# Later bits for the second head, zero products in the head, and output tiles in the activation buffers: a bucketed attention with two feed-forward layers

## The chip, the cores and the metric

The kernel runs on one core of a Trainium2 chip. The metric is the device time of one execution in microseconds. Three runs of the kernel before took 791.81, 792.76 and 794.22 us; the median, 792.76, stands for it.

## The reference

Three stages follow each other. The attention has 2 batches of 8 heads, 768 tokens and 64 features a head. A query attends only to the keys in its own bucket; a bucket is the pattern of the signs of six projections. Two feed-forward layers of 1536 tokens x 512 features x 2048 hidden units come behind it, with different activations.

```python
q_bits = (einsum('bhsd,dk->bhsk', q, proj) > 0)         # the same for k
mask = q_bucket[..., :, None] == k_bucket[..., None, :]  # bucket = sum(bits * 2**i)
scores = where(mask, q @ k.T / sqrt(64), -1e9)
attn = exp(scores - max); attn = attn / (sum(attn) + 1e-9)
x = (attn @ v)                                  # heads side by side: 1536 x 512
h = x @ moe_w_in;  x = (h * tanh(softplus(h))) @ moe_w_out
h = x @ moe2_w_in; out = (h - tanh(h)) @ moe2_w_out
```

## The kernel before, in words

All products are split: every operand is kept as a high part in TensorE's rounded float format and a low part that holds the rest, and high x high, low x high and high x low are summed.

*Attention.* Heads are taken in eight pairs. For a pair, `load` brings k, q and v, `halves_split` makes the high and low parts (ql, kl and so on), and `piece` multiplies them by the projection planes (L412 to L414, three matmuls into a PSUM tile y). `bits` then turns y into signs: on VectorE for k, on ScalarE for q (L397, L395). The signs of both heads go into a tile z. For the first pair alone, the first head's signs are also written directly into its operand tiles (c and d, by a second `bits` on the same y), and `first_stack` copies the rest of that head's operands on the engines. All other heads get their operands a, b, c, d by DMAs from these tiles (`stack`), issued from SyncE; d<-z and c<-z are the two that need z.

A head is worked off in two halves of the queries, a half in three tiles of 128 queries. `scores` multiplies (L507, L508) into the PSUM tile s, of which there is one; VectorE clamps it and takes its minimum (L511), and ScalarE takes the exponential and its sum (L533). Scores 1, 3 and 5 of the whole program (`SPLIT_S`) use two single-bank PSUM tiles instead. `chunk` is called for six chunks of 128 keys a half: three transposes (L554) put the chunk into a PSUM tile pt, ScalarE casts it to the high part ph (L567), VectorE forms the low part pl (L570), or GpSimd does both for a few chunks (L559, L563), and two matmuls multiply ph and pl by the values (L578, L579). There are three tiles each for ph and pl, two for GpSimd's chunks, and six PSUM tiles with the tag pt, which y, the transposes, the products' sum and later the hidden layer share. `gather` adds the two halves of a product's rows (L586, L589), and `finish` divides by the sums (rden, L602 and L607) and splits the result into xh and xl.

*Feed-forward.* `feed_forward` goes over three blocks of 512 tokens for each layer; a block takes 16 hidden tiles: `hidden` (12 matmuls, L756 to L758), the activation (`mish`, or `shrink` with tanh into an f buffer, L791), the split into ph and pl, and `outer` (12 matmuls, L815) into four sums; two of these are the halves of s. In the second layer the sums are copied to osb buffers, of which there are two (L865, the last tile in two halves, L862), and stored. `convert` turns the double-precision weights into high and low float parts on VectorE, ScalarE and GpSimd.

*The order.* Each piece of work is an `op` with an engine, a booked cost, a key and the tiles it reads and writes. `Plan.order` lays all ops out by these costs: on each engine the one that can start first, and among equals the one with the lowest key. A result is taken to reach another engine after a booked latency (`LATE`, 0.25 us, for ScalarE, VectorE and GpSimd); `release` holds an op back to a time of this plan. The instructions are then written in that order, and each engine works its own list strictly in it. Keys are times too: chunk c of item n has `at(6n + c)`, a tick being 1.16 us, and a product had the key of its chunk plus `PV_LAG` = 4.0.

Ahead of the plan, VectorE clears a tile and casts it into `hot`, and seven matmuls of zeros (L900, `WARM`) run on TensorE.

Of the kernel before, what the change touches and what calls it, by code (L numbers as in the profile page):

```python
# [27 lines left out]
F32 = mybir.dt.float32  # L28
# [15 lines left out]
POOL_LAST = ((4,), (4,))  # L44
SPLIT_S = (1, 3, 5)
TAIL = 3
WARM = 7


G_BUFS, E_BUFS, GX_BUFS, F_BUFS = 3, 3, 2, 4  # L50
T_BUFS, O_BUFS, P_BUFS, U_BUFS = 3, 2, 6, 3

EPS = 0.005
SPARE = 1
LATE = 0.25
LATS = 0.15
LATC = 1.0
LATG = 0.6  # L60
# [5 lines left out]
T_ATT = 6.0  # L66
M0 = 6.0
AHEAD = 8
PV_LAG = 4.0
PIECE = 2.5  # L70
STACK = 11
VALUES = 11
# [1 line left out]
FIRST = (0.0, 1.0, 2.0, 6.0)  # L74
V_REL = 14.0
Q_REL = 8.0
OUT_LAG = 13.0
RAW = 12.0
C0 = 6.0
# [28 lines left out]
class Plan:  # L108
# [11 lines left out]
    def buf(self, pool, tag, shape, dtype=F32):  # L120
        return Buf(self, pool, tag, shape, dtype)
# [107 lines left out]
def tile_lsh_attention_moe(  # L229
# [63 lines left out]
    )  # L293
    ctx.enter_context(
        memory("left", (
            ("const", "", 1), ("xy", "", 1), ("wa", slots(0, N_A), 1), ("osb", "osb", O_BUFS), ("t", "t", T_BUFS),
            ("g", "ph", G_BUFS), ("e", "pl", E_BUFS), ("f", "f", F_BUFS),
        ))
    )
# [9 lines left out]
    xh = [xy_p.tile([P, B * S], F32R, name=f"xh{kk}") for kk in range(KD)]  # L309
    xl = [xy_p.tile([P, B * S], F32R, name=f"xl{kk}") for kk in range(KD)]  # L310

    zero = plan.pools["osb"].tile([P, XB], F32, tag="osb", name="zero")
    hot = plan.pools["osb"].tile([P, XB], F32R, tag="osb", name="hot")

    def x_tok(which, kk, t0, n):
        return [(which, kk, t) for t in range(t0, t0 + n)]
# [16 lines left out]
    def at(tick):  # L333
        return T_ATT + tick * TICK
# [57 lines left out]
    def bits(nm, out, y, r):  # L392

        if nm == "q":
            nc.scalar.activation(out=out, in_=y[r, :HB], func=AF.Sign, bias=zb[r], scale=-1.0)  # L395
        else:
            nc.vector.tensor_scalar(  # L397
                out=out, in0=y[r, :HB], scalar1=zb[r], scalar2=zs[r], op0=ALU.is_gt, op1=ALU.mult
            )

    def piece(g, nm, half, key):

        if (g, "z") not in stacks:
            stacks[g, "z"] = buf("z", "z", [64, S], F32R)
        z, (th, tl) = stacks[g, "z"], stacks[g, nm]
        c = slice(half * HB, (half + 1) * HB)
        y = buf("ps_t", "pt", [P, 512])
        r0 = 0 if nm == "k" else 32

        def planes():  # L410
            o = y()[:64, :HB]
            nc.tensor.matmul(o, pjh, th()[:, c], start=True, stop=False)  # L412
            nc.tensor.matmul(o, pjl, th()[:, c], start=False, stop=False)
            nc.tensor.matmul(o, pjh, tl()[:, c], start=False, stop=True)  # L414

        op("PE", 0.53, key + 0.3, planes, [(th, half), (tl, half)], [y])
        eng, cost = ("ACT", 0.55) if nm == "q" else ("DVE", 0.59)
        if g == 0:
            dst = stacks[0, 0][3 if nm == "k" else 2]
            rb = slice(r0, r0 + NR)  # L420
            op(eng, cost, key + 0.4, lambda: bits(nm, dst()[0:NR, c], y(), rb), [y], [(dst, "bits", half)])
        r = slice(r0, r0 + 2 * NR)
        op(eng, cost, key + 0.4, lambda: bits(nm, z()[r, c], y(), r), [y], [(z, nm, half)])

    def stack(g, h, key):

# [47 lines left out]

    def values_in(g, h, key):
        vt = buf("vt", "vt", [P, NT, 2 * D], F32R)
        hi, lo = (slice(0, D), slice(D, 2 * D))[::1 if h == 0 else -1]
        raw = raws[g, "v"]
        op(
            "POOL", 0.5, key, lambda: pool_copy(vt()[:, :, hi], raw()[:, h]), [raw], [(vt, 0)],  # L480
            release=0.0 if g else V_REL,
        )
        op(
            "POOL", 0.97, key + 0.1,
            lambda: nc.gpsimd.tensor_tensor(
                out=vt()[:, :, lo], in0=raw()[:, h], in1=vt()[:, :, hi], op=ALU.subtract
            ),
            [raw, (vt, 0)], [(vt, 1)],
        )
        vts[g, h] = vt  # L490
# [47 lines left out]
        )  # L538
        return p

    def chunk(g, h, half, c, ps, o, key):
# [9 lines left out]
        def transpose():  # L551
            for t in range(TB):
                pc = ps[t]().rearrange("p a b -> p (a b)")
                nc.tensor.transpose(pt()[:, t * P:(t + 1) * P], pc[:, c * P:(c + 1) * P], ident)  # L554

        op("PE", 0.41, key, transpose, ps, [pt])
        if pooled:
            pf = buf("f", "f", [P, XB])
            op("ACT", 0.38, key + 0.1, lambda: nc.scalar.copy(pf()[:, w], pt()[:, :HB]), [pt], [pf])  # L559
            op("POOL", 0.5, key + 0.2, lambda: pool_copy(ph()[:, w], pf()[:, w]), [pf], [ph], lat=LATG)  # L560
            op(
                "POOL", 0.97, key + 0.3,
                lambda: nc.gpsimd.tensor_tensor(out=pl()[:, w], in0=pf()[:, w], in1=ph()[:, w], op=ALU.subtract),  # L563
                [pf, ph], [pl], lat=LATG,
            )
        else:
            op("ACT", 0.38, key + 0.1, lambda: nc.scalar.copy(ph()[:, w], pt()[:, :HB]), [pt], [ph])  # L567
            op(
                "DVE", 0.47, key + 0.2,
                lambda: nc.vector.tensor_tensor(  # L570
                    out=pl()[:, w], in0=pt()[:, :HB], in1=ph()[:, w], op=ALU.subtract
                ),
                [pt, ph], [pl],
            )

        def product():
            vc = vt()[:, c, :]
            nc.tensor.matmul(o()[:, :HB], vc, ph()[:, w], start=(c == 0), stop=False)  # L578
            nc.tensor.matmul(o()[:, :HB], vc, pl()[:, w], start=False, stop=(c == NT - 1))  # L579

        op("PE", 0.35, key + PV_LAG, product, [(vt, 0), (vt, 1), ph, pl], [o])

    def gather(h, o, u, key):
        main, rest = slice(h * D, (h + 1) * D), slice((1 - h) * D, (2 - h) * D)
# [55 lines left out]
    for g in range(len(pairs)):  # L640
        load(g)
        k0 = at(TICKS * (g - 1)) if g else 0.0
        if g == 0:
            clear_stack()
        else:
            for n, nm in enumerate("kq"):
                halves_split(g, nm, (0, 1), k0 + PIECE * n * TICK)
        for n, (nm, half) in enumerate((("k", 0), ("q", 0), ("k", 1), ("q", 1))):
            key = k0 + PIECE * n * TICK if g else FIRST[n]
            if g == 0:  # L650
                halves_split(0, nm, (half,), key)
            piece(g, nm, half, key)
            if g == 0:
                first_stack(half, nm, key + 0.35)
        for h in range(2):
            if g or h:
                stack(g, h, k0 + STACK * TICK if g else 5.0)
            values_in(g, h, k0 + (VALUES + 2 * h) * TICK)
        us = []
        for half in range(2):  # L660
            sums[g, half] = buf("small", "sums", [P, 2, TB])
            us.append(buf("u", "u", [P, HB]))
        for h in range(2):
            for half in range(2):
                n = (2 * g + h) * 2 + half
                ps = [
                    scores(g, h, half, t, at(NT * n + 2 * t - AHEAD) + 0.3) for t in range(TB)
                ]
                o = buf("ps_t", "pt", [P, 512])
                for c in range(NT):  # L670
                    chunk(g, h, half, c, ps, o, at(NT * n + c))
                gather(h, o, us[half], at(NT * (n + 1)) + PV_LAG)
                if h == 1:
                    finish(g, half, us[half], at(NT * (n + 1)) + PV_LAG + 0.3)


    wb_es = ExitStack()
# [144 lines left out]
    def feed_forward(which, j, first):  # L822
# [17 lines left out]
        for d, (a, n) in enumerate(acc):  # L840
# [13 lines left out]
            else:  # L854
                b, t = divmod(j * TX + d, NT)
                rows = out[b * S:(b + 1) * S, :].rearrange("(t p) d -> t p d", p=P)[t]
                osb = buf("osb", "osb", [P, DM])
                eng, cost, e = (("ACT", 0.48, nc.scalar.copy), ("DVE", 0.6, nc.vector.tensor_copy))[d % 2]
                if tail and d == KD - 1:
                    for i in range(2):  # L860
                        c = slice(i * hm, (i + 1) * hm)
                        op("ACT", 0.26, key, lambda osb=osb, a=a, n=n, c=c: nc.scalar.copy(osb()[:, c], a()[:, n, c]), [(a, n)], [(osb, i)])  # L862
                        dma(P * hm * 4, key, lambda rows=rows, c=c: rows[:, c], lambda osb=osb, c=c: osb()[:, c], [(osb, i)], [("out", j, d, i)])
                    continue
                op(eng, cost, key, lambda osb=osb, a=a, n=n, e=e: e(osb(), a()[:, n, :]), [(a, n)], [osb])  # L865
                dma(P * DM * 4, key, lambda rows=rows: rows, osb, [osb], [("out", j, d)])
# [26 lines left out]

    nc.scalar.dma_start(out=cst, in_=cst_d)
    nc.scalar.preload_act_table_set("natural_log_exp_and_others")
    nc.vector.memset(zero, 0.0)
    nc.vector.tensor_copy(hot, zero)
    for _ in range(WARM):
        o = plan.pools["ps_t"].tile([P, XB], F32, tag="pt", name="hot_ps")
        nc.tensor.matmul(o, hot[:, 0:P], hot, start=True, stop=True)  # L900
# [61 lines left out]
```

## Time and profile before

| | us |
|---|---|
| median of three runs | 792.76 |
| the profiled execution | 792.33 |
| its span (first to last instruction) | 790.6 |
| TensorE busy in the span | 769.4 (97%) |
| VectorE busy | 489.3 (62%) |
| ScalarE busy | 408.0 (52%) |
| GpSimd busy | 302.1 (38%) |

PE is TensorE's matmul side, PEld its weight loads, DVE VectorE, ACT ScalarE, POOL GpSimd, SP SyncE; ACTq and SPq are the sides of these engines that issue DMAs. Busy shares are means over stages with different limits: attention ends near 250 us, the feed-forward layers fill the rest. Ends of matmuls are modelled, so two matmuls overlap in the listing, and the distance of two starts says what one takes. "idle before" names the event that ended an engine's wait.

### The profile page before, as it was taken

What the parts mean: (1) busy time and instruction counts of PE and PEld (TensorE: products, weight loads), DVE (VectorE), ACT (ScalarE), POOL (GpSimd) and SP (SyncE); (2) the same over time, 40 slices, a digit from 0 to 9 for tenths busy, and PEclk for the clock granted to TensorE, in tenths of its full rate; (3) what the DMA queues carried; (4) which work ended last, traced back from release to release, by engine and by line L of the source; (5) the groups of instructions that cost most, each with busy time, mean ns of one, the idle gap of its engine ahead of it and who ended that gap; (6) DMA issues with size and microseconds to landing.
All of it is one profiled execution on the core that took longest, in us unless ns stands there. A gap on an engine that the chain in (4) does not pass through costs nothing.

```text
span 790.6 us, 10579 instructions
## 1 busy us (share of the span) xinstructions
PE 769.4 (97%) x3799; PEld 647.2 (82%) x3799; DVE 489.3 (62%) x792; ACT 408.0 (52%) x799; POOL 302.1 (38%) x308
## 2 busy tenths in 40 slices
PE   7999999999998899999999999999999999999997
PEld 5799898898887788887888888888887888888886
DVE  7888888898898998862111279889832322232221
ACT  6889899899888455443121345465522222222122
POOL 4676667667658766540000056555500000000000
PEclk9999999999999999999999999999999999999999
DMA  6574474563790460000000354530000100010001
GB/s 168 138 171 110 106 165 107 114 159 85 183 353 20 185 240 1 1 0 1 1 0 27 107 212 167 208 133 1 1 0 1 54 0 1 1 53 1 1 0 54
DMA packets 23009, 65.82 MB, mean 83 GB/s; under 512 B 3494, under 2 KB 4390, under 8 KB 22956
## 3 DMA queue, kind: packets, MB, share of 16 engines
q1 hardware_dynamic: 22524, 64.65, 27.5%
q8 instruction: 30, 0.49, 0.2%
q10 hardware_dynamic: 432, 0.49, 0.2%
q14 instruction: 23, 0.19, 0.1%
HBM read 43.09 MB, written 3.15 MB: 58 GB/s over the span
## 4 chain that ended last, share of the span: by engine, by line
PE 79%; DVE 12%; ACT 5%; issue 2%; DMA 1%; POOL 0%; ACTq 0%; DVEq 0%; POOLq 0%
PE s L815 17%; PE pt L815 16%; PE pt L758 11%; PE pt L756 11%; PE pt L757 11%; DVE p L511 4%; PE s L507 3%; PE pt L554 3%; PE s L508 3%; ACT p L533 2%; DVE pl L570 2%; PE pt L579 2%; PE pt L578 2%; DVE u L589 1%; DVE z L397 1%
## 5 line engine op out<-in xcount | busy, mean ns | idle before, releaser
L758 PE MATMUL pt<-xh,wi 128*128 128x512 f32 x384 | 151.1, 394 | 2.4 <-POOL wi L740 2.4
L756 PE MATMUL pt<-xh,wi 128*128 128x512 f32 x384 | 151.0, 393 | 0.0
L757 PE MATMUL pt<-xl,wi 128*128 128x512 f32 x384 | 150.7, 393 | 0.0
L794 DVE TENSOR_TENSOR pt<-pt,f 128x512 f32<-128x512 f32 x48 | 33.4, 697 | 118.1 <-ACT f L791 118.1
L784 DVE TENSOR_TENSOR pl<-f,ph 128x512 fp32r<-128x512 f32 x48 | 47.7, 996 | 88.3 <-ACT ph L781 88.1
L732 POOL TENSOR_TENSOR t<-t,wi 128x512 uint32<-128x512 uint32 x32 | 48.0, 1499 | 133.8 <-ACT wi L727 128.0
L533 ACT ACTIVATE p<-p,mn 128x768 f32<-128x768 f32 x96 | 90.3, 941 | 15.6 <-DVE p L511 13.3
L511 DVE TENSOR_SCALAR_CACHE_REDUCE p<-s 128x768 f32<-128x768 f32 x93 | 88.2, 948 | 12.7 <-PE s L508 12.0
L780 ACT ACTIVATE f<-pt 128x512 f32<-128x512 f32 x48 | 28.7, 598 | 129.8 <-PE pt L758 129.3
L791 ACT ACTIVATE f<-pt 128x512 f32<-128x512 f32 x48 | 28.7, 598 | 126.9 <-PE pt L758 126.6
L554 PE MATMUL pt<-cst,p 128*128 128x128 f32 x576 | 89.4, 272 | 1.6 <-ACT p L533 0.9
L758 PEld LDWEIGHTS pt<-xh,wi 128*128 128x128 f32 x384 | 72.1, 188 | 19.3 <-POOL wi L740 2.8
L756 PEld LDWEIGHTS pt<-xh,wi 128*128 128x128 f32 x384 | 72.2, 188 | 16.1
L757 PEld LDWEIGHTS pt<-xl,wi 128*128 128x128 f32 x384 | 72.1, 188 | 16.0
L554 PEld LDWEIGHTS pt<-cst,p 128*128 128x128 f32 x576 | 72.2, 140 | 8.8 <-ACT p L533 1.5
L570 DVE TENSOR_TENSOR pl<-pt,ph 128x384 fp32r<-128x384 f32 x146 | 76.2, 550 | 4.8 <-ACT ph L567 4.0
L507 PE MATMUL s<-b,a 128*128 128x384 f32 x186 | 69.1, 371 | 5.5 <-DVE p L511 5.0
L578 PE MATMUL pt<-ph,vt 128*128 128x384 f32 x192 | 72.7, 379 | 1.6 <-DVE pl L570 1.0
L567 ACT CAST ph<-pt 128x384 fp32r<-128x384 f32 x146 | 67.2, 476 | 8.9 <-PE pt L554 5.9
L579 PE MATMUL pt<-pl,vt 128*128 128x384 f32 x192 | 65.9, 343 | 1.4 <-DVE pl L570 1.3
L508 PE MATMUL s<-d,c 77*128 77x384 f32 (+1 forms) x186 | 63.7, 342 | 1.1 <-DVE d L397 1.0
L732 POOL TENSOR_TENSOR t<-t,wo 128x512 uint32<-128x512 uint32 x32 | 48.2, 1508 | 36.0 <-ACT wo L727 24.0
(109 smaller groups left out, 1546.6 us busy)
## 6 DMA issues: line engine op xcount, KB each, us to landing
wi<-in_moe_w_in_dram SPq DMA_DIRECT2D x32, 512.0 KB
wo<-in_moe_w_out_dram SPq DMA_DIRECT2D x32, 512.0 KB
b<-kh SPq DMA_DIRECT2D x30, 192.0 KB
v<-in_v_dram SPq DMA_DIRECT2D x8, 384.0 KB
a<-qh SPq DMA_DIRECT2D x15, 192.0 KB
a<-ql SPq DMA_DIRECT2D x15, 192.0 KB
d<-kl SPq DMA_DIRECT2D x15, 192.0 KB
c<-qh SPq DMA_DIRECT2D x15, 192.0 KB
```

The source lines that it names most:

```text
L507: nc.tensor.matmul(o, a()[:, tok], b_()[:, kc], start=True, stop=False)
L508: nc.tensor.matmul(o, c_()[used, tok], d_()[used, kc], start=False, stop=True)
L511: nc.vector.tensor_scalar(out=out, in0=in_, scalar1=MASKED, scalar2=None, op0=ALU.min, op1=ALU.min, accum_out=low)
L533: lambda: nc.scalar.activation(out=p(), in_=p(), func=AF.Exp, bias=mn(), scale=-1.0, accum_out=sm()[:, h, t:t + 1],),
L554: nc.tensor.transpose(pt()[:, t * P:(t + 1) * P], pc[:, c * P:(c + 1) * P], ident)
L570: lambda: nc.vector.tensor_tensor(out=pl()[:, w], in0=pt()[:, :HB], in1=ph()[:, w], op=ALU.subtract),
L578: nc.tensor.matmul(o()[:, :HB], vc, ph()[:, w], start=(c == 0), stop=False)
L732: lambda: nc.gpsimd.tensor_tensor(out=t(), in0=t(), in1=word(0), op=ALU.add),
L756: nc.tensor.matmul(h(), w()[:, 0, c], xh[kk][:, cols], start=(kk == 0), stop=False)
L757: nc.tensor.matmul(h(), w()[:, 0, c], xl[kk][:, cols], start=False, stop=False)
L758: nc.tensor.matmul(h(), w()[:, 1, c], xh[kk][:, cols], start=False, stop=(kk == KD - 1))
L815: nc.tensor.matmul(o, x, y, start=st and i == 0, stop=sp and i == 2)
```

## The change

- Zero tile and warm-up: `hot` is cleared directly by VectorE and lives among the constants; nine warm-up matmuls instead of seven.
- For the first pair, the `bits` that write z get `release` 12.5 (`Z_REL`). Behind the planes of the second half of k, TensorE gets four matmuls of zeros of 384 columns (`FILL`), which may start when these planes have started.
- The products with the values are no longer ops with the key of their chunk plus 4.0 us: a queue holds them, and each call of `chunk` issues the product of the fourth chunk before it, with that chunk's key plus 0.05. `gather` and `finish` of a half follow its last product (`done`). Three transposes are booked with 0.33 us instead of 0.41, and `LATE` is 0.22.
- The second head's values keep high and low parts in the same columns as the first head's.
- The output tiles of the second layer take f buffers (four) instead of osb (two, gone). The last tile's second half is copied by VectorE instead of ScalarE, and its first half is stored by a DMA that ScalarE issues.

```diff
-WARM = 7
+WARM = 9
-T_BUFS, O_BUFS, P_BUFS, U_BUFS = 3, 2, 6, 3
+T_BUFS, P_BUFS, U_BUFS = 3, 6, 3
-LATE = 0.25
+LATE = 0.22
-PV_LAG = 4.0
+PV_LAG = 4
+Z_REL = 12.5
+FILL = 4
...
-    zero = plan.pools["osb"].tile([P, XB], F32, tag="osb", name="zero")
-    hot = plan.pools["osb"].tile([P, XB], F32R, tag="osb", name="hot")
+    hot = const.tile([P, XB], F32R, name="hot")
...
-        op("PE", 0.53, key + 0.3, planes, [(th, half), (tl, half)], [y])
+        first = op("PE", 0.53, key + 0.3, planes, [(th, half), (tl, half)], [y])
...
-        op(eng, cost, key + 0.4, lambda: bits(nm, z()[r, c], y(), r), [y], [(z, nm, half)])
+        op(eng, cost, key + 0.4, lambda: bits(nm, z()[r, c], y(), r), [y], [(z, nm, half)], release=0.0 if g else Z_REL)
+        if (g, nm, half) == (0, "k", 1):
+            o = buf("ps_t", "pt", [P, 512])
+
+            def warm():
+                for _ in range(FILL):
+                    nc.tensor.matmul(o()[:, :HB], hot[:, 0:P], hot[:, :HB], start=True, stop=True)
+
+            op("PE", 0.2 * FILL, key + 0.35, warm, [], [o], after=[first])
...
-        hi, lo = (slice(0, D), slice(D, 2 * D))[::1 if h == 0 else -1]
+        hi, lo = slice(0, D), slice(D, 2 * D)
...
+    def product(todo, key):
+
+        vt, c, ph, pl, o, done = todo
+
+        def emit():
+            nc.tensor.matmul(o()[:, :HB], vt()[:, c, :], ph()[:, :HB], start=(c == 0), stop=False)
+            nc.tensor.matmul(o()[:, :HB], vt()[:, c, :], pl()[:, :HB], start=False, stop=(c == NT - 1))
+
+        op("PE", 0.35, key, emit, [(vt, 0), (vt, 1), ph, pl], [o])
+        if done:
+            done()
+
+    queue = []
...
-        op("PE", 0.41, key, transpose, ps, [pt])
+        op("PE", 0.33, key, lambda: transpose(range(TB)), ps, [(pt, 0), (pt, 1)])
+        if len(queue) >= PV_LAG:
+            product(queue.pop(0), key + 0.05)
...
-        op("PE", 0.35, key + PV_LAG, product, [(vt, 0), (vt, 1), ph, pl], [o])
+        queue.append((vt, c, ph, pl, o, done))
...
-                osb = buf("osb", "osb", [P, DM])
+                osb = buf("f", "f", [P, DM])
...
-                        op("ACT", 0.26, key, lambda osb=osb, a=a, n=n, c=c: nc.scalar.copy(osb()[:, c], a()[:, n, c]), [(a, n)], [(osb, i)])
-                        dma(P * hm * 4, key, lambda rows=rows, c=c: rows[:, c], lambda osb=osb, c=c: osb()[:, c], [(osb, i)], [("out", j, d, i)])
+                        eng, cost, e = (("ACT", 0.26, nc.scalar.copy), ("DVE", 0.34, nc.vector.tensor_copy))[i]
+                        op(eng, cost, key, lambda osb=osb, a=a, n=n, c=c, e=e: e(osb()[:, c], a()[:, n, c]), [(a, n)], [(osb, i)])
+                        if i:
+                            dma(P * hm * 4, key, lambda rows=rows, c=c: rows[:, c], lambda osb=osb, c=c: osb()[:, c], [(osb, i)], [("out", j, d, i)])
+                        else:
+                            op(
+                                "ACT", 0.1, key + 0.1, lambda rows=rows, c=c, osb=osb: nc.scalar.dma_start(out=rows[:, c], in_=osb()[:, c]),
+                                [(osb, i)], [("out", j, d, i)], lat=3.0,
+                            )
...
-    nc.vector.memset(zero, 0.0)
-    nc.vector.tensor_copy(hot, zero)
+    nc.vector.memset(hot.bitcast(F32), 0.0)
```

## Rows read from the trace of the kernel before

**Rows 1.** Stretches: length, busy us (instructions) by engine, clock, DMA share, GB/s.
```profile
7.37:10.79 3.42, 1.95 (x8) 0.73 (x6) 3.32 (x7) 2.87 (x6) 1.26 (x3) 1.00 0.51 116
10.79:14.20 3.41, 3.26 (x10) 2.97 (x11) 3.35 (x11) 0.23 (x1) 0.75 (x2) 0.50 0.63 172
17.00:20.00 3.00, 2.31 (x17) 1.72 (x15) 2.34 (x9) 2.93 (x7) 0.43 (x1) 1.00 0.45 97
300.00:340.00 40.00, 40.00 (x174) 32.36 (x173) 34.81 (x36) 21.61 (x39) 24.39 (x18) 1.00 0.00 1
```
**Rows 2.** The chain that ended last, head: start, length (us), what.
```profile
9.15 0.67 DVE z L397
...
10.89 0.58 DVE z L397
...
14.57 2.87 ACT p L533 x6
...
17.46 0.57 ACT z L395
```
**Rows 3.** Stretches of one pair and of the passage; order PE, PEld, DVE, ACT, POOL.
```profile
102.08:131.34 29.26, 28.52 (x188) 26.49 (x187) 25.98 (x56) 25.91 (x57) 19.93 (x26) 1.00 0.55 128
245.00:270.00 25.00, 20.72 (x106) 16.98 (x105) 23.38 (x31) 15.09 (x30) 19.92 (x16) 1.00 0.11 41
```
**Rows 4.** Timeline of TensorE in attention: start, length (us), instruction [idle before].
```profile
102.57 0.49 PE L554 MATMUL pt<-cst,p 128*128 128x128 f32 x3
102.81 0.42 PE L578 MATMUL pt<-ph,vt 128*128 128x384 f32 x1
103.07 0.34 PE L579 MATMUL pt<-pl,vt 128*128 128x384 f32 x1
...
107.03 0.34 PE L579 MATMUL pt<-pl,vt 128*128 128x384 f32 x1
...
107.91 0.49 PE L554 MATMUL pt<-cst,p 128*128 128x128 f32 x3
...
121.85 0.45 PE L507 MATMUL s<-b,a 128*128 128x384 f32 x1 [0.68 <-DVE p L511]
```
**Rows 5.** Waits: us in total, times, longest; last row TensorE from 340 us.
```profile
DVE rden L602 <- ACT p L533: 7.1, 7, 1.0
...
PE s L507 <- DVE p L511: 5.0, 9, 0.7
...
PE s L815 <- DVE xl L849: 0.4, 1, 0.4
```
**Rows 6.** Timeline of the tail.
```profile
782.49 0.39 PE L815 MATMUL s<-wo,pl 128*128 128x512 f32 x1
...
782.91 0.59 ACT L865 COPY osb<-s 128x512 f32<-128x512 f32 x1 [2.87 <-PE s L815]
...
783.53 0.69 DVE L865 COPY osb<-s 128x512 f32<-128x512 f32 x1 [2.77 <-ACT osb L865]
...
785.92 0.39 PE L815 MATMUL pt<-wo,pl 128*128 128x512 f32 x1
```
**Rows 7.** The chain that ended last, tail.
```profile
784.27 2.67 DMA out_dram<-osb
...
787.12 0.37 ACT osb L862
```
**Rows 8.** Timeline of the head.
```profile
1.43 0.43 DVE L897 CAST hot<-zero 128x512 fp32r<-128x512 f32 x1
...
1.92 3.35 PE L900 MATMUL hot_ps<-hot 128*128 128x512 f32 x7 [1.92 <-DVE hot L897]
...
5.71 0.58 PE L412 MATMUL pt<-qh,pjh 128*64 128x384 f32 x1 [0.44 <-ACT qh L368]
...
13.97 0.57 ACT L395 ACTIVATE c<-pt,cst 13x384 fp32r<-13x384 f32 x1 [3.59 <-PE pt L414]
...
22.93 0.33 PE L507 MATMUL s<-b,a 128*128 128x384 f32 x1
```

More of the change, by code (lines that the diff above doesn't have):

```diff
@@ L295, in tile_lsh_attention_moe @@
         memory("left", (
-            ("const", "", 1), ("xy", "", 1), ("wa", slots(0, N_A), 1), ("osb", "osb", O_BUFS), ("t", "t", T_BUFS),
+            ("const", "", 1), ("xy", "", 1), ("wa", slots(0, N_A), 1), ("t", "t", T_BUFS),
             ("g", "ph", G_BUFS), ("e", "pl", E_BUFS), ("f", "f", F_BUFS),
@@ L539, in scores, with chunk @@
         return p
-    def chunk(g, h, half, c, ps, o, key):
+    def product(todo, key):
[7 more added lines that the diff above has]
+    queue = []
+    def chunk(g, h, half, c, ps, o, key, done):
         vt = vts[g, h]
@@ L549, in chunk, with transpose @@
         w = slice(0, HB)
-        def transpose():
-            for t in range(TB):
+        def transpose(ts):
+            for t in ts:
                 pc = ps[t]().rearrange("p a b -> p (a b)")
                 nc.tensor.transpose(pt()[:, t * P:(t + 1) * P], pc[:, c * P:(c + 1) * P], ident)
-        op("PE", 0.41, key, transpose, ps, [pt])
+        op("PE", 0.33, key, lambda: transpose(range(TB)), ps, [(pt, 0), (pt, 1)])
+        if len(queue) >= PV_LAG:
+            product(queue.pop(0), key + 0.05)
+        both = [(pt, 0), (pt, 1)]
         if pooled:
             pf = buf("f", "f", [P, XB])
-            op("ACT", 0.38, key + 0.1, lambda: nc.scalar.copy(pf()[:, w], pt()[:, :HB]), [pt], [pf])
+            op("ACT", 0.38, key + 0.1, lambda: nc.scalar.copy(pf()[:, w], pt()[:, :HB]), both, [pf])
             op("POOL", 0.5, key + 0.2, lambda: pool_copy(ph()[:, w], pf()[:, w]), [pf], [ph], lat=LATG)
@@ L566, in chunk @@
         else:
-            op("ACT", 0.38, key + 0.1, lambda: nc.scalar.copy(ph()[:, w], pt()[:, :HB]), [pt], [ph])
+            op("ACT", 0.38, key + 0.1, lambda: nc.scalar.copy(ph()[:, w], pt()[:, :HB]), both, [ph])
             op(
@@ L572, in chunk @@
                 ),
-                [pt, ph], [pl],
+                [*both, ph], [pl],
             )
[L576 to L579, printed above, removed]
-        op("PE", 0.35, key + PV_LAG, product, [(vt, 0), (vt, 1), ph, pl], [o])
+        queue.append((vt, c, ph, pl, o, done))
     def gather(h, o, u, key):
@@ L669, in tile_lsh_attention_moe, with done @@
                 o = buf("ps_t", "pt", [P, 512])
+                def done(g=g, h=h, half=half, o=o, u=us[half], key=at(NT * (n + 1)) + PV_LAG):
+                    gather(h, o, u, key)
+                    if h == 1:
+                        finish(g, half, u, key + 0.3)
                 for c in range(NT):
[L671 to L674, printed above, removed]
+                    chunk(g, h, half, c, ps, o, at(NT * n + c), done if c == NT - 1 else None)
+    for i, todo in enumerate(queue):
+        product(todo, at(n_items + i))
     wb_es = ExitStack()
```

## The prediction

> **What bounds the kernel now.** I read the time by stretches first, and in each stretch asked which engine has no idle time. From about 270 us to the last matmul TensorE is full: 40.00 of 40.00 us in the sample row [rows 1]. No part of the change touches the number or the size of its matmuls there, so these 516 us stay. What can move is the head (to 25 us), attention (25 to about 220), the passage into the feed-forward (220 to 270) and the tail after the last matmul.
>
> The head hangs on VectorE. It is busy for 3.32 of 3.42 us and then for 3.35 of 3.41, while TensorE works for 1.95 of 3.42 and then runs at a granted clock of 0.50 [rows 1]. The chain of waits stays on VectorE until 14.57 us, and two of its links, 0.67 us at 9.15 and 0.58 at 10.89, write z, the bits that only the second head of the pair reads [rows 2]. Behind 14.57 the chain is the exponentials of ScalarE, which has 2.93 of 3.00 us filled [rows 1, 2].
>
> In attention one pair of heads takes 29.26 us (the period at which the chain repeats), and TensorE is the fullest engine: 28.52, against 25.98 (VectorE) and 25.91 (ScalarE) [rows 3]. Its busy figure hides gaps, so I count by starts [rows 4]. Five matmuls of 384 columns start between 107.03 and 107.91, one every 0.176 us. Three transposes start 0.24 before the matmul behind them (102.57, 102.81), which then needs 0.26 (to 103.07), so they cost 0.24 + 0.26 - 0.176 = 0.33. A pair has 24 chunks of three transposes, 108 such matmuls (48 products, 48 scores, 12 planes) and two more groups of three transposes: 26 x 0.33 + 108 x 0.176 = 27.6 us. So 1.7 us a pair are waits. The largest is plain in the rows: 0.68 us at 121.85, for VectorE's minimum; waits of that kind sum to 5.0 us in 9 places [rows 4, 5].
>
> In the passage VectorE is the full one, 23.38 of 25.00 us [rows 3]; the change takes nothing from it there.
>
> The tail is 4.3 us behind the last matmul's end (785.92 + 0.39 = 786.31; span 790.6). The last two copies start at 787.12, because their osb buffer is one of two and waits for a transfer of 2.67 us that was issued at 784.27 [rows 6, 7].
>
> **The change part by part.** The sum is made against the profiled execution, 792.33 us with 790.6 of span; the median shown is 792.76, that is 0.43 more, and I carry the saving over to it.
>
> *Second head's bits later (Z_REL).* Four instructions move: two on VectorE and two on ScalarE (0.57 each). Of these the ScalarE one at 17.46 already stands late, so three move. VectorE's chain before the first minimum loses 0.67 + 0.58 = 1.25 us [rows 2]. They come back after planner time 12.5, where VectorE has 0.66 us idle in a stretch of 3.00 [rows 1], so its 1.25 us are hidden over some 6 us. ScalarE is nearly full there, so its moved 0.57 comes back in full. What they feed are the second head's transfers d<-z and c<-z; the latter waits already for the late one (17.46). Behind them on SP stand loads of the next pair, and the second head's first score starts at 22.93 [rows 8]. If the moved bits are done before 17.46, nobody waits. Their three plane tiles stay in PSUM for longer: three, plus two tiles of a split score, plus one of the last planes, are just the six there are. If this doesn't fit, the first scores wait and up to the whole 1.25 is lost.
>
> *Zero products and warm-up.* Four matmuls of 384 columns on TensorE are 4 x 0.176 = 0.70 us at full clock, 1.3 at half (ten take 3.26, 0.326 each) [rows 1]. The idle time there is 3.42 - 1.95 = 1.47 us, so they cost 0, at most 0.7 if a score would have been ready. What they may give: the granted clock was 1.00 from 7.37 to 10.79, with TensorE busy for those 1.95 us, and 0.50 in the next 3.41 [rows 1]. Ten matmuls there pay 0.326 - 0.176 = 0.15 each, 1.5 us, but the chain is VectorE's. Only the bits at 13.97, for which ScalarE sat idle for 3.59 us [rows 8], sit on it in part; I count 0.3. The two extra warm-up matmuls are 2 x 0.48 (3.35 / 7), the removed cast gives back 0.43, so the last of nine ends near 1.92 - 0.43 + 9 x 0.48 = 5.8, and ScalarE's first result lets the planes start at 5.71 [rows 8]: 0, or 0.1 lost.
>
> Head: 1.25 - 0.57 + 0.3 = 1.0 us gained, between 0 (PSUM full, or the ScalarE bits cost what VectorE gains) and 2.1 (all 0.57 hidden in holes, and 0.3 more from the clock).
>
> *Products by a queue, transposes booked at 0.33, LATE 0.22.* No instruction is added or removed; the written order changes. The old order was laid out with 0.41 us for three transposes. With the kernel's own bookings that makes TensorE's pair 24 x (0.41 + 0.35) + 12 x 0.7 + 4 x 0.53 + 2 x 0.41 = 29.6, more than what it executes; with 0.33 it is 27.7, near the 27.6 counted above. So the old order was laid out for a TensorE with no slack, and VectorE's queue was filled as if it had 2 us more a pair than it has. The rows show what this brings: VectorE's rden instruction stands at the head of its queue and waits for an exponential, 7.1 us in 7 places, and behind it stands the minimum for which TensorE waits [rows 5]. I expect the new order to remove about two thirds of TensorE's 5.0 us of such waits: 3.3 us, or 0.5 for each of some 6.5 pairs (the last one and a half run into the VectorE-bound passage). From both sides: all the slack would be 6.5 x 1.7 = 11.0 us gained; a new wait of 0.68 in each pair 6.5 x 0.68 = 4.4 lost. I take the value from the nearest row, the visible waits. The swapped halves of the values are the same two GpSimd instructions, and the sum that gathers them reads the same sizes: 0.
>
> *Output through the f buffers.* The copies from 787.12 on no longer wait for a transfer: the last tile's first half starts 0.03 behind the matmul (as 782.91 does behind 782.49 + 0.39), at 786.34 [rows 6]. ScalarE takes 0.37 for a half [rows 7]. VectorE's half reads the same PSUM tile. The row of such a pair shows VectorE starting at 783.53, 0.03 after ScalarE's copy from the same tile ends (782.91 + 0.59), though its matmuls were done by 782.88 [rows 6]; so I count the halves one behind the other: 786.71 + 0.03, then VectorE's 0.43 (an estimate: its 0.69 for 512 columns by ScalarE's ratio, 0.37 to 0.59 [rows 6, 7]), 787.17, 0.02 to the issue and 2.67 to landing [rows 7]: 789.86. The tail loses 790.60 - 789.86 = 0.74 us; side by side the copies would make it 1.1. The Trainium skill, "PSUM — Partial Sum Buffer", section "PSUM bank collisions raise a hardware error", says that ScalarE and VectorE may not access the same bank and partitions at once, reads included, and that schedulers put a dependency between them; by it the split can't run side by side, and the trace agrees with its 783.53. That the first half leaves from ScalarE's queue means that SP is free for the second, which is inside this sum.
> At the two earlier block ends the outputs now take f slots beside tanh's tile. Four slots are enough for the overlap in the trace (three outputs of 2.67 us each and one tanh), and TensorE waits for nothing there but 0.4 us in all from 340 us on [rows 5]: 0. If tanh came to wait for a transfer, it could cost up to 2.67 at each of two ends, 5.3 us.
>
> Sum: 1.0 + 3.3 + 0.74 = 5.0. 792.76 - 5.0 = 787.7.
>
> **The rivals.**
> *Only the ends move.* Attention keeps its 29.26 us, because the minimum, which needs the one score tile, sets the pace and not the order. For it: VectorE and ScalarE are each 89% busy [rows 3], and the wait for the minimum is the longest in a pair. Against: that wait stands behind an order laid out for another pace. 792.76 - 1.74 = 791.0.
> *The order comes out tight.* Three quarters of the slack go, 1.25 us a pair: 6.5 x 1.25 + 1.74 = 9.9, so 782.9. For it: the bookings now fit the starts. Against: the waits for an exponential [rows 5] come from ScalarE's queue too, whose bookings stay as they are.
> *Slower: products held back.* The place is the chunk's cast on ScalarE. A product is now ordered behind the transposes of the fourth chunk after it, 4 ticks of 1.16 = 4.64 us, where it had 4.0; its ph and pl tiles (three each, two for GpSimd's chunks) come free later, the cast waits for them, and in ScalarE's queue the exponentials stand behind it. For it: four chunks in flight want more than these three. Against: VectorE and ScalarE have over 3 us a pair free to catch up [rows 3]. At one wait of 0.68 in each pair [rows 4] 4.4 us are lost: 792.76 - 1.74 + 4.4 = 795.4. It decides (over 0.3%) from (2.4 + 1.74) / 6.5 = 0.64 us a pair.
> *The head does not do what it says.* The plane tiles crowd PSUM and the first scores wait: the head gives 0, and with the forecast's other terms it is 788.7, with attention unchanged 792.0.
>
> **How the numbers follow.** A difference under 0.3% (2.4 us: 790.4 to 795.1) can't be told from none. Forecast 0.47 (own range 785.5 to 790.3), only the ends 0.20, tight 0.13, products held back 0.16, head without gain 0.04. Faster: 0.47 + 0.13 + 0.02 = 0.62. The ends alone, the other half of the head's case (0.02) and the mild quarter of the held-back case (0.04) make 0.26 the same, and 0.12 is left for slower. The range, 782 to 794, holds the forecast, the ends and most of the tight case, and leaves out the worse part of the held-back one.
>
> **What would show it.** The first exponential should start near 13.3 us instead of 14.57, without z in VectorE's chain before the first minimum, and the granted clock should stay at 1.00 in 10.8 to 14.2. The pair's period should be about 28.8 us, and TensorE's waits for the minimum under 2 us in all. The last VectorE copy should start 0.03 behind ScalarE's, and the span should end 3.5 us behind the last matmul. A period of 29.3 or more, or a second head's first score later than 22.9, makes the prediction wrong.

## The result, and the profile after

The changed kernel takes 780.69 us (median of six executions, of which five lie between 780.43 and 780.77), the kernel before 792.33 beside it (six, 791.50 to 794.22). The ratio is 0.9848 [0.9834, 0.9863]: 12.0 us faster by the ratio, 11.6 by the medians. The forecast was 787.7 with a range of 782 to 794; the sign was right, the size was not, and the rival "the order comes out tight" (782.9) came nearest. The sixth, the one profiled first, ran at a mean granted clock of 0.557 from end to end (1268.38 us) and is left out of the comparison; the profile below is of an execution of the same kernel that took 780.81 us (span 779.0, mean clock 0.999).

The same stretches of the kernel after (length, then busy us and instructions of PE, PEld, DVE, ACT, POOL, then clock, DMA share, GB/s):

```profile
7.37:10.79 3.42, 2.83 (x14) 2.14 (x15) 2.79 (x6) 1.96 (x4) 1.18 (x2) 1.00 0.61 164
10.79:14.20 3.41, 2.33 (x12) 1.30 (x10) 3.38 (x11) 2.25 (x5) 0.68 (x2) 1.00 0.84 211
17.00:38.00 21.00, 20.83 (x133) 18.52 (x132) 19.54 (x49) 19.48 (x43) 14.28 (x19) 1.00 0.61 149
93.88:121.77 27.89, 27.89 (x188) 26.22 (x187) 25.60 (x56) 25.43 (x58) 19.66 (x26) 1.00 0.58 134
245.00:270.00 25.00, 24.39 (x109) 20.09 (x109) 24.00 (x27) 13.09 (x24) 17.33 (x13) 1.00 0.61 234
300.00:340.00 40.00, 40.00 (x174) 32.26 (x173) 32.20 (x35) 20.59 (x37) 25.11 (x18) 1.00 0.00 1
```

The clock stays at 1.00 in 10.79 to 14.20, where it was 0.50 (one of TensorE's two levels, 1.2 GHz, against 2.4) [rows 1]. One pair, from its first exponential to the next pair's, takes 27.89 us and TensorE is busy in all of it; it was 29.26 with 28.52 busy [rows 3]. The work is the same: 188 matmuls fall into the stretch in both. From 300 to 340 us nothing changed for TensorE, 174 matmuls in 40.00 us in both [rows 1].

Where the time went is read from marks that both traces have. The first product of the second pair and that of the seventh, before:

```profile
51.30 0.34 PE L578 MATMUL pt<-ph,vt 128*128 128x384 f32 x1
...
197.57 0.34 PE L578 MATMUL pt<-ph,vt 128*128 128x384 f32 x1
```

and after:

```profile
47.83 0.42 PE L555 MATMUL pt<-ph,vt 128*128 128x384 f32 x1
...
187.26 0.42 PE L555 MATMUL pt<-ph,vt 128*128 128x384 f32 x1
```

The first mark is 3.47 us earlier (head and first pair), the second 10.31, so the five pairs between gave 6.84, or 1.37 each. The last matmul starts at 775.13 instead of 785.92, 10.79 earlier: the last two pairs and the passage give only 0.5 more. The tail gives the rest of the 11.5 us of span: 3.9 us from that start to the end of the span, where it was 4.6. The tail's timeline after (start, length, instruction, in brackets the idle time before it and what ended it):

```profile
775.13 0.39 PE L840 MATMUL pt<-wo,pl 128*128 128x512 f32 x1
775.61 0.37 ACT L888 COPY f<-pt 128x256 f32<-128x256 f32 x1 [1.47 <-PE pt L840]
776.01 0.35 ACTq L893 DMA_DIRECT2D out_dram<-f  x1
776.01 0.42 DVE L888 COPY f<-pt 128x256 f32<-128x256 f32 x1 [2.59 <-ACT f L888]
```

No copy waits for a transfer any more, and VectorE's half starts 0.03 behind ScalarE's end (775.61 + 0.37).

The waits that the forecast counted, after (us in all, times, longest):

```profile
DVE rden L622 <- ACT p L542: 3.1, 7, 0.9
...
PE s L516 <- DVE p L520: 1.8, 4, 0.8
```

TensorE's wait for the minimum went from 5.0 us in 9 places to 1.8 in 4, and rden's from 7.1 to 3.1 [rows 5]. These waits of TensorE's matmuls fell by 3.2 us, nearly the 3.3 that the forecast took, and the time fell by far more.

### The profile page after: what moved, and what is told of

Its sections match the earlier page's. It is cut to its first block, busy times and chain, and to the rows that moved or that the text cites. A ratio compares the mean times of both kernels' runs of the same rounds, so it can differ in the third digit from the quotient of the medians.

```text
span 1266.6 us, 10616 instructions
## 1 busy us (share of the span) xinstructions
PE 1260.3 (100%) x3805; PEld 787.8 (62%) x3805; DVE 464.0 (37%) x792; ACT 409.9 (32%) x798; POOL 286.7 (23%) x308
## 4 chain that ended last, share of the span: by engine, by line
PE 99%; DVE 0%; DMA 0%; ACT 0%; issue 0%; ACTq 0%
PE pt L840 17%; PE s L840 17%; PE pt L781 12%; PE pt L782 12%; PE pt L783 12%; PE pt L577 9%; PE pt L556 4%; PE pt L555 4%; PE s L516 4%; PE s L517 4%; PE pt L415 1%; PE pt L639 1%; PE pt L413 1%; PE pt L414 1%; DMA q<-in_q_dram 0%; ACT p L542 0%
## 5 line engine op out<-in xcount | busy, mean ns | idle before, releaser
L782 PE MATMUL pt<-xl,wi 128*128 128x512 f32 x384 | 221.5, 577 | 0.0
L781 PE MATMUL pt<-xh,wi 128*128 128x512 f32 x384 | 221.2, 576 | 0.1
L783 PE MATMUL pt<-xh,wi 128*128 128x512 f32 x384 | 220.9, 575 | 0.0
L577 PE MATMUL pt<-cst,p 128*128 128x128 f32 x576 | 142.3, 386 | 0.8 <-ACT p L542 0.8
L781 PEld LDWEIGHTS pt<-xh,wi 128*128 128x128 f32 x384 | 83.6, 218 | 63.8 <-issue 37.5
L783 PEld LDWEIGHTS pt<-xh,wi 128*128 128x128 f32 x384 | 83.9, 218 | 63.1 <-issue 35.8
L555 PE MATMUL pt<-ph,vt 128*128 128x384 f32 x192 | 109.0, 568 | 0.0
L516 PE MATMUL s<-b,a 128*128 128x384 f32 x186 | 93.8, 504 | 0.0
L840 PE MATMUL s<-ph,wo 128*128 128x512 f32 x192 | 92.4, 579 | 0.0
L840 PE MATMUL pt<-ph,wo 128*128 128x512 f32 x192 | 92.3, 577 | 0.0
L840 PE MATMUL pt<-wo,ph 128*128 128x512 f32 x192 | 92.2, 576 | 0.0
L840 PE MATMUL s<-wo,ph 128*128 128x512 f32 x192 | 92.2, 577 | 0.0
```

Source lines behind the costliest of these rows:

```text
L516: nc.tensor.matmul(o, a()[:, tok], b_()[:, kc], start=True, stop=False)
L555: nc.tensor.matmul(o()[:, :HB], vt()[:, c, :], ph()[:, :HB], start=(c == 0), stop=False)
L781: nc.tensor.matmul(h(), w()[:, 0, c], xh[kk][:, cols], start=(kk == 0), stop=False)
L782: nc.tensor.matmul(h(), w()[:, 0, c], xl[kk][:, cols], start=False, stop=False)
L783: nc.tensor.matmul(h(), w()[:, 1, c], xh[kk][:, cols], start=False, stop=(kk == KD - 1))
L840: nc.tensor.matmul(o, x, y, start=st and i == 0, stop=sp and i == 2)
```

## The experiments

**The three parts alone.** Each is the kernel before with one part of the change (the head with the directly cleared `hot`, the order with the values in the same columns, the tail with the store from ScalarE's queue).

```diff
 head alone
+WARM = 9
...
+FILL = 4
...
+        op(eng, cost, key + 0.4, lambda: bits(nm, z()[r, c], y(), r), [y], [(z, nm, half)], release=0.0 if g else Z_REL)
 order alone
+LATE = 0.22
...
+        op("PE", 0.33, key, lambda: transpose(range(TB)), ps, [(pt, 0), (pt, 1)])
...
+        queue.append((vt, c, ph, pl, o, done))
 tail alone
+                osb = buf("f", "f", [P, DM])
...
+                        eng, cost, e = (("ACT", 0.26, nc.scalar.copy), ("DVE", 0.34, nc.vector.tensor_copy))[i]
```

> The changed kernel as it is, for a profile at the full clock. Theory (the order of the products and transposes carries the surplus): 780.7 us, and a pair's period near 27.9 us, that is 1.3 to 1.4 below 29.26 in some 7 pairs, with TensorE close to the 27.6 counted by starts. Rival (the head carries the surplus): the period stays above 28.5 us and the first pair's products start more than 4 us earlier.

The changed kernel again: 780.85 us, 0.9846 [0.9827, 0.9866], a pair 27.9 us.

> The kernel before with the head's edits alone (bits of z released at 12.5, four zero products, nine warm-up matmuls, hot cleared directly). Theory: 791.3 us or so, 1 to 2 us below the kernel before. Rival (head carries the surplus): 787 or less, 5 us below.

Measured: 792.77, 0.9996 [0.9986, 1.0005]: no gain clear of noise, where the theory had 1 to 2 us. The head does what it says (first exponential at 11.39 us, 14.57 in the profile before), and then loses it. Length, PE, PEld, DVE, ACT, POOL busy, clock, DMA share, GB/s of the stretch behind the head, first in the kernel before, then with the head alone:

```profile
17.00:38.00 21.00, 18.50 (x116) 15.81 (x115) 16.95 (x38) 18.42 (x41) 11.84 (x16) 1.00 0.53 132
```
```profile
17.00:38.00 21.00, 18.98 (x121) 17.17 (x120) 18.59 (x45) 18.34 (x41) 13.20 (x19) 1.00 0.51 131
```

With the whole change TensorE is busy for 20.83 of these 21.00 us, with the head alone for 18.98: under the old order TensorE is idle for 2 us right behind the head.

> The kernel before with the new order alone (products from a queue, 0.33 for three transposes, LATE 0.22, values in the same columns). Theory: 782 to 784 us, 8.5 to 10 us below the kernel before, the period near 27.9. Rival: 787 to 789, the 3.3 to 5 us of the forecast, with a period near 28.7.

Measured: 783.73, 0.9882 [0.9867, 0.9896], 9.4 us by the ratio, a pair of about 28.0 us. The order carries nearly all of it. The values' columns are in this edit too; no run takes them alone.

> The kernel before with the output tiles in the f buffers, the last tile's halves on two engines and its stores from two queues alone. Both theories: 0.7 to 0.8 us below the kernel before, 791.6; VectorE's last copy starts 0.03 behind ScalarE's. If the halves ran side by side it would be 1.1 below.

Measured: 791.27, 0.9984 [0.9974, 0.9994], 1.3 us; the interval holds the 0.74 of the forecast. Executions of one granted clock agree better: at 0.999 the tail alone takes 790.50 to 791.71 us and the kernel before 791.35 to 791.65, 0.7 apart by the medians; the head alone takes 791.06 to 791.60 there, 0.3 apart. The three parts alone sum to 0.3 + 9.4 + 1.3 = 11.0 of about 12.

**What in the order does it.** First two parts of it on the kernel before, then two single numbers of the changed kernel put back.

```diff
 booking alone, on the kernel before
-        op("PE", 0.41, key, transpose, ps, [pt])
+        op("PE", 0.33, key, transpose, ps, [pt])
 queue alone, on the kernel before (0.41 and LATE 0.25 stay)
...
-        op("PE", 0.35, key + PV_LAG, product, [(vt, 0), (vt, 1), ph, pl], [o])
+        queue.append((vt, c, ph, pl, o, done))
 changed kernel, old booking
-        op("PE", 0.33, key, lambda: transpose(range(TB)), ps, [(pt, 0), (pt, 1)])
+        op("PE", 0.41, key, lambda: transpose(range(TB)), ps, [(pt, 0), (pt, 1)])
 changed kernel, old latency
-LATE = 0.22
+LATE = 0.25
```

> The kernel before with one number changed: three transposes are booked at 0.33 us instead of 0.41 (keys, PV_LAG and LATE as before). Theory (the wrong booking made the stalls): the pair's period falls from 29.26 to 28.2 or less and the time to 783 to 785.5 us, most of the 9 us that the order alone gave. Rival (the queue, that puts a product right behind the transposes of the fourth chunk after it, made the gain): a period of 28.9 or more, 789 to 792 us.

Measured: 787.73, 0.9937 [0.9921, 0.9954]. One number, which changes no instruction, is worth 5.0 us alone. Its pairs alternate between about 28.8 and 27.9 us. That lies between the two: less than the theory's range, more than the rival's.

> The kernel before with the queue of products alone: transposes still booked at 0.41 us, LATE 0.25. Theory (booking): a period of 28.9 or more, 789 to 793 us. Rival (queue): 28.2 or less, 783 to 786 us.

Measured: 790.61, 0.9980 [0.9969, 0.9990], 1.6 us, pairs that alternate between 27.5 and 30.5 us, 29.0 in the mean.

> The changed kernel with one number put back: three transposes booked at 0.41 us. Theory (the booking must meet what the chip takes, 0.33): the pair's period rises to 28.8 or more and the time to 786 to 790 us. Rival (within the queue the booking matters little, since the order of products and transposes is fixed by it): 27.9 to 28.2, 781 to 783 us.

Measured: 791.75, 0.9994 [0.9985, 1.0004]. With everything else of the change in place, the old booking takes the whole gain back, more than the theory's range allowed, and the pair is 29.30 us, as long as the 29.26 of before. This is the run that decides it. Its pair, in the same columns as above:

```profile
98.00:127.30 29.30, 29.16 (x187) 26.08 (x187) 25.59 (x57) 25.41 (x57) 20.03 (x26) 1.00 0.55 127
```

The view of waits names none of TensorE's matmul side (PE) in this stretch, and the busy figure says 29.16 of 29.30, though the same matmuls fit into 27.89. The loss shows in the starts (TensorE's timeline, start, length, instruction):

```profile
106.35 0.34 PE L556 MATMUL pt<-pl,vt 128*128 128x384 f32 x1
106.74 0.44 PE L516 MATMUL s<-b,a 128*128 128x384 f32 x1
...
110.98 0.34 PE L556 MATMUL pt<-pl,vt 128*128 128x384 f32 x1
111.39 0.39 PE L413 MATMUL pt<-kh,pjh 128*64 128x384 f32 x1
```

A product that takes 0.176 us from start to start is followed after 0.39 and 0.41. The product's modelled end (0.34 behind its start) covers most of such a hole. What the late matmul waits for stands in the row of its weight load (PEld). The first of the two holes, with the end of VectorE's minimum ahead of it:

```profile
106.61 0.07 DVE L520 DVE_READ_ACCUMULATOR p<-s 128x1 f32 x1
...
106.74 0.19 PEld L516 LDWEIGHTS s<-b,a 128*128 128x128 f32 x1 [0.37 <-DVE p L520]
```

And all waits of the weight loads in this pair (us in all, times, longest):

```profile
PEld s L516 <- DVE p L520: 1.5, 5, 0.4
PEld pt L413 <- DVE pl L596: 0.4, 1, 0.4
```

So the holes are waits for VectorE, five of them for the minimum that frees the score tile s. In the kernel after, a whole pair (93.88 to 121.77) has one such wait of 0.3 us; in the kernel before (102.08 to 131.34) two, 1.2 us in all. In the kernel after, the same product is followed by the next start after 0.17:

```profile
94.34 0.49 PE L577 MATMUL pt<-cst,p 128*128 128x128 f32 x3
94.59 0.42 PE L555 MATMUL pt<-ph,vt 128*128 128x384 f32 x1
94.85 0.34 PE L556 MATMUL pt<-pl,vt 128*128 128x384 f32 x1
95.02 0.49 PE L577 MATMUL pt<-cst,p 128*128 128x128 f32 x3
```

It also confirms the price that the forecast counted: three transposes and the matmul behind them, 94.34 to 94.85, take 0.51, less 0.176 is 0.33.

> The changed kernel with LATE put back to 0.25. Theory (booking and queue make the gain): 780.5 to 782 us, a period of 27.9 to 28.1. Rival (the shorter latency has a part of the 9 us of the order): 783 us or more, a period of 28.3 or more.

Measured: 785.02, 0.9908 [0.9893, 0.9923]: 0.03 us of booked latency is worth 4.2 us (785.02 - 780.85). The pairs alternate, 27.65 and 29.04 us. In some places a matmul of the planes, which needs a free PSUM tile, now waits for VectorE to have formed a chunk's low part from one:

```profile
107.73 0.49 PE L577 MATMUL pt<-cst,p 128*128 128x128 f32 x3
108.41 0.39 PE L413 MATMUL pt<-kh,pjh 128*64 128x384 f32 x1 [0.20 <-DVE pl L596]
```

**Is it the fit of the booking, or a lucky order?** If a booking pays because it meets what the chip takes, its neighbours must pay too, and a booking too low must lose as one too high does. If the order was lucky, neighbours should scatter.

```diff
 changed kernel, transposes booked 0.25 (then 0.31, 0.35)
-        op("PE", 0.33, key, lambda: transpose(range(TB)), ps, [(pt, 0), (pt, 1)])
+        op("PE", 0.25, key, lambda: transpose(range(TB)), ps, [(pt, 0), (pt, 1)])
 changed kernel, LATE 0.20 (then 0.24)
-LATE = 0.22
+LATE = 0.20
```

> The changed kernel with three transposes booked at 0.25 us, as far below what the chip takes as 0.41 is above. Theory (booking must meet it): the order is stale the other way, a period of 28.2 or more and 783 us or more. Rival (the lower the booking, the more TensorE's list runs ahead and the better): a period of 27.9 or less, 780.8 us or less.

> The changed kernel with three transposes booked at 0.31 us. Theory (the booking must meet the chip's 0.33): a neighbour is nearly as good, 780.5 to 783 us, a period under 28.2. Rival (each small change lays out another order, good or bad by chance): anywhere from 781 to 790, with no relation to the distance from 0.33.

> The changed kernel with three transposes booked at 0.35 us. Theory: 780.5 to 784 us, between the changed kernel and the 791.75 of 0.41, a period under 28.4. Rival: anywhere from 781 to 790.

Measured, by booking (a pair is a fifth of the distance between the two marks used above, the first product of the second pair and of the seventh):

| transposes booked | median us | ratio | a pair, us |
|---|---|---|---|
| 0.25 | 788.16 | 0.9947 [0.9932, 0.9961] | 28.94 |
| 0.31 | 781.69 | 0.9868 [0.9840, 0.9897] | 27.87 |
| 0.33 (the change) | 780.85 | 0.9846 [0.9827, 0.9866] | 27.89 |
| 0.35 | 781.82 | 0.9870 [0.9841, 0.9899] | 28.16 |
| 0.41 | 791.75 | 0.9994 [0.9985, 1.0004] | 29.29 |

From 0.31 to 0.35, around what three transposes take by their starts, the intervals overlap and no floor can be told from another; 0.25 and 0.41 lose clearly. That speaks for the fit and against luck, with five points.

> The changed kernel with LATE 0.20. Theory: close to the changed kernel, 780 to 783 us. Rival (chance): as far from it as LATE 0.25 was, which cost 4.2 us, or farther, either way.

> The changed kernel with LATE 0.24. Theory: between the changed kernel (780.7) and the one with 0.25 (785.0). Rival (chance): outside of these two.

Measured: 779.43, 0.9840 [0.9811, 0.9868] with 0.20, and 780.80, 0.9857 [0.9828, 0.9886] with 0.24; pairs of 27.8 and 27.9 us. So 0.20 to 0.24 lie within 1.5 us, 0.20 a little under its theory's range, and 0.25 is a step of 4 us. 0.20 is the fastest kernel measured here, 12.5 us below the kernel before in its own comparison (791.88); that it beats the change is not shown, the intervals overlap and each comes from two executions.

**The head inside the new order.**

```diff
 bits of z not held back
-        op(eng, cost, key + 0.4, lambda: bits(nm, z()[r, c], y(), r), [y], [(z, nm, half)], release=0.0 if g else Z_REL)
+        op(eng, cost, key + 0.4, lambda: bits(nm, z()[r, c], y(), r), [y], [(z, nm, half)])
 no zero products (the tile is still taken, so the order stays)
-                for _ in range(FILL):
-                    nc.tensor.matmul(o()[:, :HB], hot[:, 0:P], hot[:, :HB], start=True, stop=True)
+                o()
```

> The changed kernel with the bits of z of the first pair not held back. Theory (the bits' 1.25 us stand in VectorE's chain ahead of the first minimum, of which 0.57 comes back): 781.4 to 782.2 us, 0.7 to 1.4 above the changed kernel, its first minimum 1.2 us later. Rival (the gain is eaten further on, as in the head's edits alone): 780.6 to 781.0, no difference, although the first minimum is 1.2 us later.

Measured: 782.46, 0.9874 [0.9860, 0.9889]: the later bits are worth 1.6 us here, a little above the theory's range; in the old order the whole head gives 0.3 at most. The first exponential moves from 11.49 to 12.88 us. The profile of this run has a stretch of 3.42 us at a granted clock of 0.50, from 21.18 us, and its execution took 783.21; the three others, at 1.00, took 782.25 to 782.66, which leaves 1.4 to 1.8.

> The changed kernel without the four zero products (everything else stays in the same order). Theory (the zero products keep the granted clock at 1.00 in the head): the clock falls to 0.50 for some 3.4 us between 7 and 25 us, 781.3 to 782.3 us. Rival (clock does not fall, or VectorE hides it): 780.4 to 781.0 us.

Measured: 780.88, 0.9854 [0.9839, 0.9869]: nothing. The clock keeps its upper level without them (same columns as above):

```profile
7.37:10.79 3.42, 2.38 (x10) 1.40 (x11) 2.79 (x6) 2.01 (x4) 1.23 (x2) 1.00 0.63 166
10.79:14.20 3.41, 2.32 (x12) 1.30 (x10) 3.38 (x11) 2.20 (x5) 0.52 (x2) 1.00 0.92 196
```

**The split of the last tile.**

```diff
-                        eng, cost, e = (("ACT", 0.26, nc.scalar.copy), ("DVE", 0.34, nc.vector.tensor_copy))[i]
+                        eng, cost, e = ("ACT", 0.26, nc.scalar.copy)
```

> The changed kernel with both halves of the last tile copied by ScalarE again, the two queues kept. Theory (VectorE's half waits for ScalarE's read of the same PSUM tile): the second half ends 0.1 to 0.2 us earlier than VectorE's, 780.6 us, and the span ends 3.3 to 3.4 us behind the last matmul's end. Rival (the halves overlap in the changed kernel): it ends 0.25 later.

Measured: 780.90, 0.9855 [0.9835, 0.9875]. ScalarE does both halves in one go:

```profile
775.32 0.39 PE L840 MATMUL pt<-wo,pl 128*128 128x512 f32 x1
775.80 0.65 ACT L888 COPY f<-pt 128x256 f32<-128x256 f32 x2 [1.47 <-PE pt L840]
```

The second half is done 0.74 us behind the matmul's end (775.71) instead of 0.91 (775.52 to 776.43), and the time does not show it. VectorE's help there is worth nothing; what the tail gained is the buffer that is free and, perhaps, the second queue, which no run separates.

## Why the prediction was right and wrong

*The order (forecast 3.3, measured 9.4 alone).* This is the step that failed: the size of TensorE's waits for VectorE's minimum. The forecast counted 1.7 us of slack a pair, by starts, and that count was right: 29.26 - 27.6, of which the change took 1.37 in each of the five middle pairs, to 27.89. It then did not use the count. It took the waits that the trace names for the matmuls, 5.0 us in 9 places, and two thirds of them, 0.5 a pair, as the part that an order can remove, and the 1.7 as a bound "from both sides". The wait was the right one, and its price was too low, because a late start under a modelled end is not named in the matmuls' rows. The rows of the weight loads name it. All waits of weight loads for the minimum (us, times, longest), before, after, and with the booking of 0.41:

```profile
PEld s L507 <- DVE p L511: 11.1, 24, 0.9
...
PEld s L516 <- DVE p L520: 5.6, 12, 1.1
...
PEld s L516 <- DVE p L520: 13.8, 38, 0.9
```

The matmuls' own rows, and VectorE's rden, with the booking of 0.41:

```profile
PE s L516 <- DVE p L520: 2.0, 6, 0.6
...
DVE rden L622 <- ACT p L542: 2.2, 6, 0.4
```

| kernel | median us | weight loads wait for the minimum, us (times) | matmuls wait for it, us (times) |
|---|---|---|---|
| before | 792.33 | 11.1 (24) | 5.0 (9) |
| 0.41 in the changed kernel | 791.75 | 13.8 (38) | 2.0 (6) |
| queue alone | 790.61 | 10.5 (27) | 2.5 (8) |
| 0.25 booked | 788.16 | 8.1 (25) | 1.1 (3) |
| booking alone | 787.73 | 6.6 (17) | 2.4 (7) |
| order alone | 783.73 | 5.8 (13) | 1.8 (4) |
| the change | 780.85 | 5.6 (12) | 1.8 (4) |

The column of the weight loads goes with the time, the column of the matmuls does not. Over all 17 kernels measured, the weight loads wait 6.6 us or more in those above 787 us and 5.9 or less in those below 786; the matmuls' waits overlap (1.1 to 5.4 above, 0.6 to 1.9 below). (A weight load's wait is longer than the delay of its matmul: 0.37 for 0.21 at 106.74.) One link of the forecast does not hold: rden's wait for an exponential is shorter with 0.41 (2.2 us) than in the changed kernel (3.1), so it is not what makes the minimum late there; what does is open. The rival at 1.25 a pair had the right size; it got a chance of 0.13 because ScalarE's bookings stay as they are, and no run shows these to matter.

What the forecast argued about the cause holds at its start: the old order was laid out for a TensorE with no slack. The booking decides (0.41 undoes everything), and bookings near 0.33 are the good ones. The change of `LATE`, 4.2 us of the total when undone, had no term of its own in the sum. The numbers don't add up one by one: 0.33 alone gives 5.0 and the queue alone 1.6, but taken out of the whole, 0.33 costs 11 and 0.22 costs 4.

*The head (forecast 1.0).* The later bits measured 1.6 with the new order, the whole head 0 to 0.3 with the old. The sum took it as independent of the order, and there it failed, if by little. z is gone from VectorE's chain before the first minimum, as forecast; the chain that ended last, at the head, after (start, length, what):

```profile
10.49 0.75 DVE p L520
...
11.37 1.04 DVE p L520 x5
12.41 0.47 DVE ql L379
...
12.98 0.90 ACT p L542
...
13.92 1.01 ACT p L542 x2
14.95 0.57 ACT z L396
15.55 0.57 ACT c L396
```

The first exponential starts 3.1 us earlier (14.57 to 11.49), not 1.25, but 1.7 of that is not the change's. The four kernels above that keep the old head (order alone, tail alone, booking alone, queue alone) start it at 12.81 to 12.97. The tail alone shows where the difference lies, its chain first, then a row of ScalarE's timeline:

```profile
8.66 0.67 DVE z L397
...
10.40 0.58 DVE z L397
...
11.45 1.84 DVE p L511 x6
```
```profile
12.21 0.57 ACT L395 ACTIVATE c<-pt,cst 13x384 fp32r<-13x384 f32 x1 [2.33 <-PE pt L414]
```

Its z links are the same, and 0.5 us earlier (8.66 for 9.15): the first transfer of q, which heads both chains, took 3.42 us against 3.91. The other 1.2 us are the half-clock stretch: in ScalarE's queue the bits c stand ahead of the first exponential and wait for the planes, and they start at 12.21 here and at 13.97 in the profile before [rows 8], where the planes ran at 0.50.

So the half-clock stretch of the profile before belonged to that execution. Without it the new head gives 1.4 (12.88 to 11.49 in the two runs of the new order). That this is close to the 1.25 counted is in part luck: VectorE's first minimum starts 0.96 us earlier (11.45 to 10.49), and the rest comes from the bits c, which the forecast did not move and which are now ordered behind the first exponentials (12.28 to 15.55). The moved bits come back on ScalarE, as forecast: z at 14.95. The second head's first score starts at 21.33 us, not later than the 22.93 of before [rows 8].

*The zero products (forecast 0, with 0.3 for the clock).* They cost nothing and give nothing: 780.88 without them. The 0.3 rested on the half-clock stretch of one execution. The mean granted clock over all executions does suggest a gain of another kind: beside the run of the change again, the kernel before took 791.35 to 791.65 us in executions at 0.999 and 791.92 to 793.65 in those at 0.994 to 0.998, while the five counted of the change are at 0.999 or 1.00. So about 1 us of the 12 may be half-clock stretches that the change avoids; no run isolates it.

*The tail (forecast 0.74).* Measured 0.73 between the traces, by the steps forecast: the copies come one behind the other. The Trainium skill, "PSUM — Partial Sum Buffer", section "PSUM bank collisions raise a hardware error", says that ScalarE and VectorE may not use one bank and partitions at once; the trace agrees, with VectorE's start at 776.01, behind ScalarE's end at 775.98. The 783.53 that the forecast brought for it shows less: there the two engines copy different halves of s, a whole sum of 512 columns each, and VectorE waits all the same. The waits are shown, their reason is not.

*The passage and the f buffers (forecast 0).* TensorE's busy time in 245 to 270 us rises from 20.72 [rows 3] to 24.39, since the stretch now holds work from some 10 us further on. VectorE is nearly full in it both times (23.38 and 24.00 of 25.00). The one wait of 2.4 us for a GpSimd conversion in the kernel before's passage is gone after, and the last two pairs and the passage together still gain only 0.5. No output tile waits at the two earlier block ends.

*Held-back products.* The rival with a price of 4.4 us lost did not come: the wait itself did, since in a pair the casts wait 0.7 us in 3 places for the first of two products to release ph, where it was 0.2 in one, but the period does not show it (27.89).

*Open.* Why 0.25 of latency makes a step of 4 us where 0.24 makes none is not settled; the planes that wait for a PSUM tile are where it can be seen. Why the minimum comes late in VectorE's queue with 0.41 is open too. That the last two pairs give nothing is only located: the seventh pair, from 197.57 to 225.44, took 27.87 us in the kernel before already, and takes 28.13 after.

## What to carry to other kernels

When an order is laid out by booked costs, book what one operation adds from start to start on the full engine, and scan that number by small steps to both sides: here 0.08 us on one booking was worth 11 us of 792. Size the slack of a full engine by counting starts over one period, not by the waits named in its matmuls' rows, and look for the reason of a late matmul in the row of its weight load. When the bookings come to fit, expect most of the counted slack to go: here 1.37 of 1.7 us a pair. An earlier start of the first stage was worth 0.3 us at most while the order behind it left the same engine idle, and 1.6 with the order that did not.

## What was not expected of the hardware

A single stretch at a granted clock of 0.50, of 3.41 or 3.42 us, comes at different places: at 10.79 in the profile before, at 21.83 with the order alone, at 22.00 with the booking alone, at 21.18 in the changed kernel without the hold on z, at 239.66 in the one with LATE 0.24, and, ahead of the last matmul, nowhere with the queue alone, the head alone or after. In the tail-alone kernel it comes at 268.26, behind a stretch with little work for TensorE (length, busy by engine, clock, DMA share, GB/s):

```profile
264.00:268.26 4.26, 1.84 (x8) 1.22 (x7) 4.26 (x4) 1.11 (x2) 4.26 (x3) 1.00 0.46 173
268.26:271.67 3.41, 3.41 (x9) 2.64 (x9) 3.35 (x4) 1.56 (x3) 2.07 (x2) 0.50 0.89 305
```

So one profile's half-clock stretch is no term for a sum before a second profile shows it in the same place.
